# Relu on either of two engines, weighted sums in row halves, and a new order for a fused attention and FFT-gate kernel

## The chip, the cores and the metric

The kernel runs on one core of one Trainium2 chip. The metric is the device time of one execution in microseconds; of several runs the median is given. The core has five engines that work side by side: TensorE (PE, matrix products), VectorE (DVE) and ScalarE (ACT) for elementwise work, GpSimd (POOL) and SyncE (SP), which here start DMAs.

## The reference

For each of 8 batches, with S = 3136 rows, 256 columns and keys of width 64:

```python
scores = (1.0 / S) * np.matmul(z, z.transpose(0, 2, 1))   # z: 8 x 3136 x 64
attn = np.maximum(scores, 0.0) ** 2
x = u * np.matmul(attn, v)                                # u, v: 8 x 3136 x 256

proj = x @ w_proj                                         # 256 x 768
x1, x2, x3 = proj[..., :D], proj[..., D:2*D], proj[..., 2*D:]
X2 = np.fft.rfft(x2, n=S, axis=1)
H = np.fft.rfft(filter_fft, n=S, axis=0)[None, :, :]
y = x1 * np.fft.irfft(X2 * H, n=S, axis=1) * x3
out = y @ w_out
```

All inputs and the output are float32.

## The kernel before

The sequence is cut into 25 tiles of 128 rows (the last has 64) and 7 chunks of columns (five of 512, one of 256, one of 320). A unit is one batch, one chunk and up to four tiles, mostly two. For a unit, PE makes the scores (`score_mm`) into one of three pairs of PSUM banks (`ps_s`). The keys are only 64 wide, so z is kept twice, in the upper and the lower 64 rows, and two score matmuls run side by side on the two row halves of the array. Then `relu` takes the scores out of PSUM into a float32 tile `R_t`, which returns the pair, and `sq` squares `R_t` into the bf16 tile `A_t`. Then PE multiplies `A_t` with v on all 128 rows into two accumulators, `ps_o0` and `ps_o1`, one for each half of the 256 columns (`weigh`). Scores are symmetric, so some squares are transposed by DMA (`mirror`, tiles `M_t`, `M2e_t`, `M2o_t`) and used a second time in place of new scores. The last 64 rows are weighed in half-row matmuls inside score runs (`weigh_short`, which is L1681 in the profile through the helper `by_rows`).

At the end of a chunk DVE multiplies the sums with u (`xT_t`), and the projections follow (`ps_s<-xT_t,wp`), the gates (`gate_t`), and the first step of a Fourier transform of length 3136 = 64 x 49, which goes through DRAM (`spec`) twice. Per batch there are eight transform steps forward and eight inverse, with 64-row matmuls and a product with the filter spectrum H on DVE, and then the last transform step, the gating (`yT_t`) and the output projection.

A planner in the kernel's own code lays out the order before any instruction is emitted. Every piece of work is a `Task` with engines that may run it, assumed costs (`c_act`, `c_dve`, `c_pe`), dependencies and buffer slots. Two strings written out in the code fix what the planner does not choose:

- `ORDER` has one letter for each step on PE: S scores, Q transform steps, W weighted sums on 128 rows, w the first and v the second phase of a weighted sum by row halves, A, B and Z the rest. S, Q, w and v are 64-row work. The string of before holds no w and no v, though the planner knows them.
- `ENGINES` has one letter, a (ACT) or d (DVE), for each task that either engine may do, in the order in which the tasks are made. Before, these are most squares and the evacuations of PSUM; a relu is always on ACT, and the squares of the first chunk behind its first two are always on DVE.

In a w, the row halves 0 and 1 add to different accumulators at the same time (`weigh_rows`); in its v they swap. Where a row half adds to an accumulator that the other half wrote last, `by_rows` puts a wait ahead of it:

```python
dh, at = h ^ flip, slice(h * N1, (h + 1) * N1)
by_rows(
    dh, h, laid(un, acc[dh][ds(m, p), :cw]), row(v16[b], t)[at, ds(dh * P + m, p)], block(un, i, at),
    start=False, stop=False,
)
```

The planner charges 0.096 us for each crossing between 64-row and 128-row work, and 0.235 us (`TURN`) from one phase to the swapped one. Within a DMA's assumed time, constants such as `LATE_TURN` stand for the landing.

The lines of the profile that matter here: L540 every matmul, L1873 the relu, L1880 and L1882 the square on ACT and on DVE, L573 and L577 the evacuations on ACT and on DVE, L1924 the product with u, L1288 the product with H, L1382 the gating, L1681 the half-row sums.

Of the kernel before, what the change touches and what calls it, by code (L numbers as in the profile page):

```python
# [44 lines left out]
    "ASSWBAWSSWAWSASSWSWWSSSWSWSSWWSSSWWWWSWWWWSSSWWWWASSAAWASAAWSAAWWWWWSSWWWWSSBWAWAAAWAWAAWBWSSSWWAWWS"  # L45
    "SSWBWWSBBWWWWBWSSWBWWWAAWSSSWAWBWWAABWWWSSSWWAWWWSSSWWWAWAAAWAAWBASSAAWWSSSWWWWSWWBWWWBWASWWAAWSSWWS"
    "SWABAWWWWASSWAWWAWASSWWAWAWSSSWBAWWSSWAWWBWWAWWSSWAWWAWASSWAWASSAWASSWWSSAWWAQSWWQSSWWWWWQSSWWAAAWAW"
    "SQWAASWAWSSSWAWWQSQWWWSSSWWWWWQSSWWAAWAAAWAWQSSWAWAWSQSWWWWSSSWWWWQSWWWWWWQQQWAASSWAWSAAAWQQWSSQWWWW"
    "WAWASSWAWWASSAWAAAWSSQWAWSQSWWWWAWQSWSWSQWWWWQQSWWWAAWWWASQWWAAAWSQWWWAAWWSSSWWWAAAWSSSWWAWSSSWWSWSS"
    "WWWWSSWWWSWBWBWBWSSSWAAWAASSWAAWASSWBBAWWSSSWWWBWBAWWBSSWAWBWAWSSSWWBBWBWBWBBSSABAWWWBWWBWAAASWAWWWA"  # L50
    "BWSSBWABAWSSABWABAQSSWAWQSWAWSQSWWWWABWBWQSWWAASAWAAWWQSSWABAWSSQWAWQQSWWWSSSWWWWWQSSWWAAWAWAWAQSAWB"
    "QSSWAWAWWQSQWWWWWWSWSWQAWAWWWASSWAWAAWSQSWWAWWASQWWSSWWAASSWWAWWAWSSWSSWWSSWWSSWWWWSSWWBWWWABWSSSWAA"
    "WAASSWBAWBSSBWBAWWSSSWWWWWWSSBAWWABWWAAWSSSWBWBBSBBWAAAWASSBWBSAWBWAWSSWBWBWBWWBAWAAWBWBASABASQBWWAA"
    "BWSQSWWWSSQWWWWWWQSSWWAAAWAWAAWQSSWAABWSSQWWABWSSQWWWWSSQWWWSSSWWWAAWWAAWQSQWAAQSWAWWAWSSQWWWSQWWWSW"
    "QSWWWAWWAAAWWASAWSQAWAWWQSWWSSWWAASSWWWWSSSWAWSSSWWWWWWSSWWWSSWWWBWBABWSSSWAWAAASSWAAWAASSWBBWWABWSS"
    "SWWWWWSSBAWWBWWAASSWABWAASSBWBBAWABAWSSSWBWWBWBWWWSSWWAABWASSWAAAWABWSSQWAWWSBWSQSWBBWBWWWBWWSSQWWAA"
    "AWWSQBAWASQAWBWABWSSQWAWBWQSSWWWWSQSWWWSQSWWWAAAWAAWSQSWAAWWQSSWWAWWWSQSWWWWQQSWWWWWAASQAWAWAAQSWAWA"
    "WWWWSSSWWWAAWAWSSSWWAWSSSWWSSWWWWSSSWWWWWBSBWBWWSSSWAWAASSWAAWBASSWABBWBWWSSSWWAWBAWBWSSABWBWAWBABWA"
    "AAWSSSWAWBSSAWBWWBBWBWAWSSSWWWWSSWAWAWAAAWSSSWABBWABWBBAWQSSWWBWWBWSSQWWWQSWAAWWWASAAWQSABWAWSQSWAWQ"
    "SSWWWWWQSSWWWWSQBWAAWWQSAAWAWQSSWASAWWQSSWWWQQSWWWWWSQWAWAWAWAWWAAWSSQWWAAWWQSSWWWWWSSWWSSWWASSWWSSS"  # L60
    "WWWAWWWWWSSWAAWWWSSWABWSSBAWAAWSSSWBBWSAAWAAWWASSWABWWBBWWBWWAWWSSAAWASSAWABWSSSWABWSSSWBBWWABBWWBWA"
    "BWWWSSSWWBAAWWASSAAAWSQSWBBBWSQSWWWBWWWAWBBWAWQSWBAWASSWWAWSQQWAAWSQSWBAAWWQSWWBWABWSQSWWWWSSQWWWAAW"
    "SQAAWQSAWAAWSQSWAWWSSQWWWWSQSWWWQSWWAWAWAWAAWWQSSWAAWWSSSWWWAWWSSAWWAAWSSWAWSSSWWSWWWSSWWWWWSSSWWBWW"
    "BWBAWSSSWAWASSWAAAWAAWSSSWWWWBWWBBWBWBSSWBAAWWSSSWWAABWSSSWBBWAWAWBBWSSWBWBWWSSSWWAAWWBWBAAWSSQWWWQS"
    "BBWWSQSWWBBWWWWSQSWWBAWWZAWSQSWBABWWSQWSSSWABWWQSQWWWWWBWSSSWAWAWAWQSQWAWWSSQWWQSSWWWWSSSWWWZWWZWWQW"
    "AWSQWQSAAWWWWSSSWWWAWWQSSWWWWWSSSWAWWWWWWAWWWZZAAZAAZZBBBZZBBBZZBBZZZZZZQBQBZBBBQQQQQQQQBQQQQQZQZZZZ"
    "ZZZZZZZBZZZZZZZBZBBBBBBBBBBBBBBBBBBBBBBBBBBBB"
# [3 lines left out]
    "aaddddddddaadddddaaaddddaaddadadadddaadaadaaadaaaadddddddddddaaddadaaadadaddaaadaaadaddaddadaaadddaa"  # L71
    "adadaaaaaaaaddadadddadadaddaddaddddddadadadaaaaddadddaaddadadaaadadddaaadddaaaaddadaddddadaddadddada"
    "aaadddaaaaaaaddddddaddadddaaadaaaaaadadaaaaadaadddddadaddaaaaaaddaaaaddddddddddaaadadaaadaaddddaddaa"
    "addaadaadaaadadadaddadaaaaaddddadadaddddadaadaddddaadddaaaaadaddadddddaadaaadaadaaddaadadaaddaddaada"
    "daaddadaadaaadaadaddddadddaddddaaaddaadaddadddddaddadddaaaaddadaaadaaadadaddddddadaddddaaddaddaaddad"
    "daaaaaaaaaaddadaddddaaadadaaaaadadaddaaaadaaaadaaadadadadaaaadadaadadddddadadadadadddaaaaaaddadadadd"
    "dadddaaadaadadadadddaaaaaddddadaddaddddadaaaaddddaaddaaaadaaadadddadaddadddaadaaaadadaaddaadaaaadaaa"
    "daadadaaaaadaaaddddddddddaaaaaddadddadddaddadadadadddaadddaaaaaaaaaadaaaadadddadadadddadaaaddaaaaaad"
    "adadddddddddaaadaadaaaadadaadadadaaddaaaaddaaaaaaaadadddaaaaddadaddddadadadadadadadadadadaaaadaaddaa"
    "dadddadaadaaaaadaadadddadadaddadddadddaadaddadadddddaaadaaaaadaddadaadaaadaadaddddaaadaaadaadaddaaaa"  # L80
    "daaaaaddaddadaadddddadddaddadddaaddaaddddaadaadddaddaaaaaddaaaadaadaddddadaddaaddaaddadddadaddddadad"
    "daaaadadaaaaaaaaaaaadddadadaaadadadddaaddaaaaaadaaddaadddadaadddaddaadddaaaadaaaaaaaadaaaaaaaadaaaaa"
    "daaaaaaaaaaaadadddaaaaa"
# [14 lines left out]
def c_dve2(n):  # L98
    return 0.068 + n * 0.00052

# [103 lines left out]
class Task:  # L204


    def __init__(self, emit, cost, deps=(), takes=(), prio=0, lat=None, moves=0.0, late=0.0):
        self.emit, self.cost, self.takes, self.prio = emit, cost, list(takes), prio
        self.lat, self.moves, self.late = lat, moves, late
        self.deps = [d if isinstance(d, tuple) else (d, None) for d in deps]  # L210
        self.kids, self.frees = [], []
        self.left = len(self.deps)
        self.ready = 0.0
        self.end = None
        self.holders = 1
        self.second, self.split, self.flips, self.flip = None, False, False, None
        for d, _ in self.deps:
            d.kids.append(self)
# [9 lines left out]
class Plan:  # L228


    def __init__(self):
        self.free = {e: 0.0 for e in ("PE", "ACT", "DVE", "SP", "POOL")}
        self.queues = {"S": [], "Q": [], "W": [], "FA": [], "FB": [], "FZ": []}
        self.pend = {e: [] for e in ("ACT", "DVE", "SP", "POOL")}
        self.mode = None
        self.quarters = False
        self.flip, self.parted, self.turned = None, True, 0.0
        self.rest = []
        self.n = self.at = 0
        self.tasks = []  # L240
        self.spare = []
        self.pairs = None
        self.bus = 0.0

# [31 lines left out]
    def run(self, task, engine, start):  # L276
# [6 lines left out]
        task.end = end  # L283
        task.emit(engine)
# [41 lines left out]
    def pick(self, e):  # L326
        t = self.free[e]
        best = None
        for task in self.pend[e]:
            s = max(t, self.ready_at(task))  # L330
            key = (round(s / 0.03), task.prio, task.no) if s < INF else None
# [79 lines left out]
def kernel(  # L411
# [838 lines left out]
    def add_spectrum(b, puts, early=0):  # L1250
# [10 lines left out]
        for g in range(NJ // 2):  # L1261
# [34 lines left out]
            w_ = on("DVE", lambda mul=mul: mul(0), cost, evs, prio=ZP)  # L1296
            w_ = on("DVE", lambda mul=mul: mul(1), cost, [w_], prio=ZP, lat=ZL)
            z_ = w_ if final else on("DVE", add, 2 * c_dve2(2 * D), [w_], prio=ZP)

# [214 lines left out]
    def casts_at(b, c):  # L1514
# [3 lines left out]
        if n < B and 0 <= i < 4:  # L1518
            t0, t1 = ((0, 8), (8, 16), (16, 22), (22, NT))[i]

            def go_z(tick_):
# [22 lines left out]
                d = on("DVE", dup, c_dve2(P * (t1 - t0)), [a], [zd_p.slots], prio=2)  # L1544
                d.frees.append((a, 0))
# [49 lines left out]
    def m_pool(c, a):  # L1595
        return M_p[0] if a == c + 1 else M_p[1 + c % 2]
# [102 lines left out]
    w_first, w_last = {}, {}  # L1699
# [21 lines left out]
    def add_weigh(un, data, done):  # L1721
        global_k = len(plans[un[:2]])

        def part(dhs):
# [4 lines left out]
            deps = [*data, *cv[b]] if b > 0 and c == 0 else [*data]  # L1729
            t = pe(  # L1730
# [34 lines left out]
    def add_mirrored(un):  # L1765
# [6 lines left out]
        def done(t):  # L1772
            if last:
                t.frees.append((made[0], 0))
# [3 lines left out]
    def mirror(un, q_):  # L1778
# [13 lines left out]
        for a, i, ts in runs:  # L1792
# [3 lines left out]
            def go(a=a, i=i, ts=ts, rows=rows):  # L1796
# [12 lines left out]
                [] if made else [m_pool(c, a).slots], moves=0.78 * len(ts) * cw / 512, late=LATE_TURN,  # L1809
# [26 lines left out]
    for gi, g in enumerate(groups):  # L1836
# [24 lines left out]
        for i, un in enumerate(g):  # L1861
# [8 lines left out]
            def relu(un=un, rows=rows, n=n, cw=cw, box=box):  # L1870
                box["R"] = R_p.tile()
                p = blocks(live[un], n, cw)[:rows]
                has_read(nc.scalar.activation(blocks(box["R"], n, cw)[:rows], p, AF.Relu), p)  # L1873

            def sq(e, un=un, rows=rows, n=n, cw=cw, box=box, a_p=a_p):
# [5 lines left out]
                else:  # L1881
                    nc.vector.tensor_tensor(a, r, r, ALU.mult)  # L1882
# [7 lines left out]
            q_ = job(None, sq, how, [r_], [a_p.slots], prio=1)  # L1890
            q_.frees.append((r_, 0))
# [126 lines left out]
```

## Time and profile before

| | |
|---|---|
| median of 3 runs | 977.86 us (975.88 to 980.27) |
| the profiled execution | 977.09 us, its span 975.3 us |
| PE matmul, weight load | 942.9 us (97%), 468.5 us (48%) |
| DVE, ACT, POOL | 830.5 us (85%), 859.5 us (88%), 201.0 us (21%) |
| granted clock of PE | 0.997 |
| HBM | 147 GB/s over the span |

A row of the profile names the line, the engine and the operation, what is written and read with its shape, the count, the busy time in us and the mean of one in ns, and the idle time of the engine just before with what ended it. In a timeline the first two numbers are the start and the length in us. A matmul's end is modelled, so its pace is read from start to start.

### The profile page before, as it was taken

What the parts mean: (1) busy time and instruction counts of PE and PEld (TensorE: products, weight loads), DVE (VectorE), ACT (ScalarE), POOL (GpSimd) and SP (SyncE); (2) the same over time, 40 slices, a digit from 0 to 9 for tenths busy, and PEclk for the clock granted to TensorE, in tenths of its full rate; (3) what the DMA queues carried; (4) which work ended last, traced back from release to release, by engine and by line L of the source; (5) the groups of instructions that cost most, each with busy time, mean ns of one, the idle gap of its engine ahead of it and who ended that gap; (6) DMA issues with size and microseconds to landing.
All of it is one profiled execution on the core that took longest, in us unless ns stands there. A gap on an engine that the chain in (4) does not pass through costs nothing.

```text
span 975.3 us, 19343 instructions
## 1 busy us (share of the span) xinstructions
PE 942.9 (97%) x6664; PEld 468.5 (48%) x6765; DVE 830.5 (85%) x1492; ACT 859.5 (88%) x1161; POOL 201.0 (21%) x426
## 2 busy tenths in 40 slices
PE   6999999999999999999999999999999999999986
PEld 2344544355544545445444465444545455544654
DVE  8875788999899987898978997799888998889896
ACT  6788898999789999899988999899989999899783
POOL 5142311222012311213111130113201322000031
PEclk9999999999999999999999999999999999999998
DMA  9899899968998788997799997998979977896677
GB/s 156 147 173 176 119 176 159 186 127 152 182 219 176 137 185 179 212 175 151 148 207 189 180 150 173 207 198 155 155 157 206 213 155 152 188 207 143 164 208 241
DMA packets 332403, 170.31 MB, mean 175 GB/s; under 512 B 242598, under 2 KB 307942, under 8 KB 332304
## 3 DMA queue, kind: packets, MB, share of 16 engines
q1 hardware_dynamic: 302496, 132.43, 63.3%
q0 software_dynamic: 29168, 35.13, 24.0%
q10 hardware_dynamic: 640, 1.51, 0.5%
q8 instruction: 53, 0.87, 0.4%
q14 instruction: 46, 0.38, 0.1%
HBM read 90.26 MB, written 53.35 MB: 147 GB/s over the span
## 4 chain that ended last, share of the span: by engine, by line
PE 89%; DVE 4%; ACT 2%; DMA 2%; issue 2%; SPq 0%; ACTq 0%; DVEq 0%
PE ps_o_t L540 51%; PE ps_s L540 36%; ACT R_t L1873 1%; DVE A_t L1882 1%; PE ps_o_t L1681 1%; DMA conv_in_t<-spec 1%; DMA spec_in_t<-spec 1%; DVE yT_t L1382 1%; DMA M2e_t<-A_t 1%; DVE xh L1288 1%; DVE R_t L1288 0%; ACT A_t L1880 0%; DVE gate_t L1196 0%; PE ps_s L543 0%; DVE xT_t L1924 0%
## 5 line engine op out<-in xcount | busy, mean ns | idle before, releaser
L1873 ACT ACTIVATE R_t<-ps_s 128x1024 f32<-128x1024 f32 (+4 forms) x512 | 467.1, 963 | 54.2 <-PE ps_s L540 50.9
L540 PE MATMUL ps_o_t<-A_t,v_t 128*128 128x512 bf16 (+2 forms) x1936 | 441.4, 354 | 10.8 <-issue 4.4
L540 PEld LDWEIGHTS <-v_t 128*128 128x128 bf16 x2706 | 242.8, 98 | 255.2 <-issue 76.9
L1882 DVE TENSOR_TENSOR A_t<-R_t 128x1024 bf16<-128x1024 f32 (+2 forms) x274 | 300.4, 1112 | 30.4 <-ACT R_t L1873 27.1
L1880 ACT ACTIVATE A_t<-R_t 128x1024 bf16<-128x1024 f32 (+4 forms) x222 | 222.3, 1019 | 1.9 <-DMA M2e_t<-A_t 0.9
L540 PE MATMUL ps_s<-zT_t 64*128 64x512 bf16 (+5 forms) x1418 | 161.9, 356 | 1.9 <-DVE zT_t L577 0.5
L623 POOL COPY tick<-xT_t 1x1 bf16<-1x1 bf16 x54 | 14.7, 272 | 688.3 <-DVE xT_t L1924 688.3
L540 PE MATMUL ps_s<-xT_t,wp 128*128 128x512 bf16 (+2 forms) x411 | 104.5, 352 | 1.1 <-DVE gate_t L1196 0.5
L1924 DVE SCALAR_TENSOR_TENSOR xT_t<-ps_o_t,uT_t 128x256 bf16<-128x256 f32 (+2 forms) x224 | 76.0, 382 | 23.1 <-PE ps_o_t L540 18.3
L540 PEld LDWEIGHTS <-zT_t 64*64 64x64 bf16 (+1 forms) x1451 | 50.8, 100 | 91.9 <-issue 77.9
L573 ACT ACTIVATE x_t<-ps_s 128x512 bf16<-128x512 f32 (+2 forms) x126 | 71.8, 587 | 16.5 <-PE ps_s L540 14.7
L1196 DVE TENSOR_TENSOR gate_t<-ps_s,x_t 128x256 bf16<-128x256 f32 (+2 forms) x212 | 71.4, 383 | 17.4 <-PE ps_s L540 12.9
L1288 DVE TENSOR_TENSOR xh<-xh,H 128x1024 bf16<-128x1024 bf16 x120 | 82.1, 684 | 2.7 <-ACT xh L573 1.3
L540 PE MATMUL ps_o_t<-M_t,v_t 128*128 128x512 bf16 (+2 forms) x352 | 81.7, 353 | 0.0
L1382 DVE TENSOR_TENSOR yT_t<-ps_s,gate_t 128x512 bf16<-128x512 f32 (+2 forms) x95 | 57.0, 623 | 12.0 <-PE ps_s L540 11.6
L577 DVE CAST x_t<-ps_s 128x512 bf16<-128x512 f32 (+2 forms) x85 | 52.2, 623 | 12.3 <-PE ps_s L540 6.5
L614 POOL DMA_DIRECT2D un_t<-in_u_dram x112 | 59.9, 557 | 7.6 <-issue 5.7
L540 PEld LDWEIGHTS <-wp 128*128 128x128 bf16 x448 | 41.8, 98 | 39.6 <-issue 7.3
L633 POOL DMA_DIRECT2D v_t<-in_v_dram x112 | 59.4, 555 | 5.2 <-issue 1.9
L540 PE MATMUL ps_s<-wp,xT_t 128*128 128x256 bf16 x396 | 58.0, 273 | 0.2
L540 PE MATMUL ps_s<-wo,yT_t 128*128 128x256 bf16 (+1 forms) x360 | 54.3, 273 | 0.3 <-DVE yT_t L1382 0.2
L577 DVE CAST xh<-ps_s 128x512 bf16<-128x512 f32 x64 | 42.5, 684 | 8.7 <-PE ps_s L540 8.7
(166 smaller groups left out, 871.5 us busy)
## 6 DMA issues: line engine op xcount, KB each, us to landing
out_dram<-ost_t SPq DMA_DIRECT2D x60, 256.0 KB
spec<-s_t SPq DMA_DIRECT2D x96, 128.0 KB
spec_in_t<-spec SPq DMA_DIRECT2D x56, 192.0 KB
spec<-gs_t SPq DMA_DIRECT2D x56, 192.0 KB
v_t<-in_v_dram POOLq DMA_DIRECT2D x80, 128.0 KB, 5.0
un_t<-in_u_dram POOLq DMA_DIRECT2D x80, 128.0 KB, 5.4
conv_in_t<-spec SPq DMA_DIRECT2D x34, 256.0 KB
out_dram<-ost_t SPq DMA_DIRECT2D x18, 128.0 KB
```

The lines of the kernel that those rows point to most:

```text
L540: wrote(nc.tensor.matmul(o, *args, **kw), o)
L573: got = nc.scalar.activation(out_, in_, AF.Copy)
L577: got = nc.vector.tensor_copy(out_, in_)
L614: nc.gpsimd.dma_start(out=t[ds(j * N1, N1), lo - t0 : hi - t0, :], in_=x[:, n2 : n2 + hi - lo, :])
L633: nc.gpsimd.dma_start(out=t[ds(j * N1, N1), ds(v_at(a), (b - a) * D)], in_=r[:, n2 + a - lo : n2 + b - lo, :].rearrange("p t d -> p (t d)"),)
L1196: got = nc.vector.tensor_tensor(g[:, ::-1] if h == 0 else g, p, x, ALU.mult)
L1288: nc.vector.tensor_tensor(x[:, 1 - i], x[:, 0], h, ALU.mult)
L1382: got = nc.vector.tensor_tensor(yb["y"][:, dh, 0:w], p, gates[b, c, dh][:, 0:w], ALU.mult)
L1873: has_read(nc.scalar.activation(blocks(box["R"], n, cw)[:rows], p, AF.Relu), p)
L1880: nc.scalar.activation(a, r, AF.Square)
L1882: nc.vector.tensor_tensor(a, r, r, ALU.mult)
L1924: nc.vector.scalar_tensor_tensor(x, f, inv_s2, ut, ALU.mult, ALU.mult)
```

## The change

- A relu may run on ACT or DVE. `ENGINES` gains a letter for each of the 512 relus, and 11 for squares of the first chunk that were fixed on DVE (1223 to 1746 letters).
- `ORDER` is a new string: 58 W become w, with 58 v (2245 to 2303 letters).
- Three rules of the planner change: a chunk's last weighted sum comes behind the second phases; a mirror's buffer is held until all its weighted sums have read it; and a mirror in the first chunk of the first batch is assumed to land 2.0 us later.
- GpSimd gets a price for a square, but is taken off the list again in the next line; `ports` and `port` are read only for GpSimd squares.

The two strings are shown by their first line only:

```diff
 ORDER = (
-    "ASSWBAWSSWAWSASSWSWWSSSWSWSSWWSSSWWWWSWWWWSSSWWWWASSAAWASAAWSAAWWWWWSSWWWWSSBWAWAAAWAWAAWBWSSSWWAWWS"
...
+    "ASBSWASWSWASWwSASvWSwSSWvwSSvSWSwSvSWWWWSSWWWWSSWWWWWSwSvSAWSAAAWAWAWWWBWSSWWAWWSAWWBSSAWWBSSwSvwSvA"
...
 ENGINES = (
-    "aaddddddddaadddddaaaddddaaddadadadddaadaadaaadaaaadddddddddddaaddadaaadadaddaaadaaadaddaddadaaadddaa"
...
+    "aaddddddddaaadddadaaaaaaadadaadaddaaadaadaaaaadadadadadadadadadaaadddaaddaaadddaadaaadaddaaddaaadaaa"
...
+def c_pool(n):
+    return 0.12 + n * 0.00173
...
+            if k == len(plans[b, c]) - 1:
+                deps += [(x, ISSUED) for x in seconds.get((b, c), ())]
...
+                seconds.setdefault((b, c), []).append(after_it)
...
         def done(t):
-            if last:
-                t.frees.append((made[0], 0))
+            if not last:
+                made[0].holders += 1
+            t.frees.append((made[0], 0))
...
-                [] if made else [m_pool(c, a).slots], moves=0.78 * len(ts) * cw / 512, late=LATE_TURN,
+                [] if made else [m_pool(c, a).slots], moves=0.78 * len(ts) * cw / 512, late=LATE_TURN + 2.0 * (b == c == 0),
...
-            def relu(un=un, rows=rows, n=n, cw=cw, box=box):
+            def relu(e, un=un, rows=rows, n=n, cw=cw, box=box):
                 box["R"] = R_p.tile()
                 p = blocks(live[un], n, cw)[:rows]
-                has_read(nc.scalar.activation(blocks(box["R"], n, cw)[:rows], p, AF.Relu), p)
+                r = blocks(box["R"], n, cw)[:rows]
+                if e == "ACT":
+                    has_read(nc.scalar.activation(r, p, AF.Relu), p)
+                else:
+                    has_read(nc.vector.tensor_single_scalar(r, p, 0.0, ALU.max), p)
...
-            r_ = on(
-                "ACT", relu, c_act(n * cw), [(st, -sum(costs[i + 1 :]) - extra)], [R_p.slots], prio=0
+            r_ = job(
+                None, relu, both(n * cw), [(st, -sum(costs[i + 1 :]) - extra)], [R_p.slots], prio=0
             )
...
-            how = {"DVE": c_dve(n * cw)} if (b, c) == (0, 0) and k > 1 else {"DVE": c_dve(n * cw), "ACT": c_act(n * cw) + 0.039}
+            how = {"DVE": c_dve(n * cw), "ACT": c_act(n * cw) + 0.039, "POOL": c_pool(n * cw)}
+            del how["POOL"]
```

More of the change, by code (lines that the diff above doesn't have):

```diff
@@ L50 @@
[L50 to L64, printed above, removed]
@@ L68 @@
+    "BBB"
 )
 ENGINES = (
-    "aaddddddddaadddddaaaddddaaddadadadddaadaadaaadaaaadddddddddddaaddadaaadadaddaaadaaadaddaddadaaadddaa"
[L72 to L80, printed above, removed]
@@ L215, in __init__ @@
         self.holders = 1
+        self.ports = ()
         self.second, self.split, self.flips, self.flip = None, False, False, None
@@ L243, in __init__ @@
         self.bus = 0.0
+        self.port = {"DVE": 0.0, "POOL": 0.0}
     def add(self, task, kind=None):
@@ L283, in run @@
         task.end = end
+        if engine in task.ports:
+            self.port[engine] = end
         task.emit(engine)
@@ L330, in pick @@
             s = max(t, self.ready_at(task))
+            if e in task.ports:
+                s = max(s, self.port["POOL" if e == "DVE" else "DVE"])
             key = (round(s / 0.03), task.prio, task.no) if s < INF else None
@@ L1544, in go_z @@
                 d = on("DVE", dup, c_dve2(P * (t1 - t0)), [a], [zd_p.slots], prio=2)
+                d.ports = ("DVE",)
                 d.frees.append((a, 0))
@@ L1697, in weigh_rows @@
                     )
-    w_first, w_last = {}, {}
+    w_first, w_last, seconds = {}, {}, {}
     def weigh(un, dhs):
```

55 lines of the change are left out of this document (44 added, 11 removed).

## The prediction

> **What bounds the kernel now.** I read the page first: the busy shares, then the chain that ended last.
>
> ```profile
> span 975.3 us, 19343 instructions
> PE 942.9 (97%) x6664; PEld 468.5 (48%) x6765; DVE 830.5 (85%) x1492; ACT 859.5 (88%) x1161; POOL 201.0 (21%) x426
> PE 89%; DVE 4%; ACT 2%; DMA 2%; issue 2%; SPq 0%; ACTq 0%; DVEq 0%
> ```
>
> TensorE (PE) works 97% of the span and holds 89% of the chain. VectorE (DVE) and ScalarE (ACT) are near 86% each, so they are busy but not the bound on average. An average can hide a stage, so I asked for the busy time by stage, cut at the first matmul, at the end of the set-up, and at the end of the score work:
>
> ```profile
> 0.00:4.00 4.00, 0.00 (x0) 0.00 (x0) 2.28 (x18) 1.34 (x2) 3.27 (x13) 1.00 0.43 80
> 4.00:30.00 26.00, 21.75 (x110) 8.13 (x112) 21.05 (x40) 19.50 (x27) 10.00 (x24) 1.00 1.20 173
> 30.00:60.00 30.00, 28.21 (x146) 12.03 (x150) 27.64 (x52) 24.56 (x32) 7.50 (x15) 1.00 0.85 142
> 60.00:915.00 855.00, 846.31 (x5937) 418.53 (x6029) 732.29 (x1290) 780.34 (x1041) 168.01 (x353) 1.00 0.88 173
> 915.00:976.00 61.00, 46.65 (x476) 29.79 (x476) 47.27 (x97) 33.71 (x65) 12.26 (x23) 0.95 0.75 225
> ```
>
> After the length of the stage, the columns are PE, weight loads, DVE, ACT and POOL. From 60 to 915 us PE is idle for 8.7 of 855 us: seven eighths of the kernel run at PE's own pace, and shifting work between ACT and DVE cannot shorten them unless PE itself gets less to do. The idle time of PE that could go is 4.2 us before 30, 1.8 us before 60, 8.7 us in the middle, and 14.4 us after 915, the last of which includes the stores after the final matmul.
>
> Whether "busy" hides stalls is seen from start to start in PE's timeline:
>
> ```profile
> 264.56 1.89 PE L540 MATMUL ps_o_t<-A_t,v_t 128*128 128x512 bf16 x8
> 266.29 0.39 PE L540 MATMUL ps_s<-T,conv_in_t 128*128 128x128 bf16 x4
> ...
> 275.38 1.03 PE L540 MATMUL ps_o_t<-M_t,v_t 128*128 128x512 bf16 x4
> 276.34 0.61 PE L540 MATMUL ps_s<-zT_t 64*128 64x512 bf16 x4
> 276.88 0.61 PE L540 MATMUL ps_s<-xT_t,wp 128*128 128x512 bf16 x2
> ...
> 262.50 0.39 PE L540 MATMUL ps_s<-zT_t 64*128 64x512 bf16 x2
> 262.73 0.38 PE L1681 MATMUL ps_o_t<-As_t,v_t 64*128 64x512 bf16 x2
> 262.94 0.38 PE L540 MATMUL ps_s<-zT_t 64*128 64x512 bf16 x2
> 263.25 0.61 PE L540 MATMUL ps_s<-xT_t,wp 128*128 128x512 bf16 x2
> ```
>
> Eight full matmuls take 266.29 - 264.56 = 1.73 us, 0.216 each, which is the pace. Four of them would take 0.86 us, but the score run behind 275.38 starts after 0.96: crossing from 128 rows to 64 rows costs 0.10. Its four matmuls go two at a time (2 x 0.216 = 0.43), and the next full matmul starts after 0.54: crossing back costs 0.11. So a run of 64-row work costs about 0.2 us in crossings, whatever it holds. The rows at 262.73 are a weighted sum by row halves inside such a run: 0.23 and 0.21 us from start to start for a pair, no more than the score pairs around it.
>
> **The change, part by part.**
>
> *Fewer crossings.* In the string ORDER the letters S, Q, w, v are 64-row work and the rest is full. Counting changes between the two kinds gives 548 before and 528 after (274 and 264 runs). That is 20 x 0.10 = 2.0 us less, directly on PE. The matmul work itself does not change: a weighted sum of two tiles is four full matmuls, 4 x 0.216 = 0.86 us, and as two phases it is four pairs, also 4 x 0.216.
>
> *The phases.* 58 of the 928 weighted-sum steps become a w and a v. The second phase lets each row half add to the sum that the other half has just written, and it waits for that. Following the string, the halves swap within a run 26 times: 13 times with one score or transform unit between, 13 times with two or more; never with none. In 22 other cases the second phase begins in a new run, behind full matmuls, and in the remaining 10 it meets no swap. The trace of before has no swap. Its nearest bound from below is 0 (the pair at 262.73 shows no premium); from above it is the part of a matmul that outlasts the pace, 0.38 - 0.216 = 0.16 us, with no cover by the unit between: 26 x 0.16 = 4.2 us. I take 0.8 us, nearer to zero, because a unit of 0.216 lies between and is longer than the 0.16.
>
> [...]
>
> *Relus and squares.* I walked the steps in the order in which the code makes them and read the two engine strings along. Of 512 relus, 161 go to DVE (120 of 1024 elements, 32 of 640, 9 smaller). 93 squares go the other way, from DVE to ACT (DVE 286 to 193), and 52 evacuations net as well.
>
> ```profile
> L1873 ACT ACTIVATE R_t<-ps_s 128x1024 f32<-128x1024 f32 x408 | 403.0, 1035 | 47.8 <-PE ps_s L540 45.2 <-DVE xh L577 0.5 <-DVE A_t L1882 0.5
> L1873 ACT ACTIVATE R_t<-ps_s 128x640 f32<-128x640 f32 x72 | 47.9, 710 | 4.9 <-PE ps_s L540 4.3 <-DVE xT_t L1924 0.2
> L1882 DVE TENSOR_TENSOR A_t<-R_t 128x1024 bf16<-128x1024 f32 x208 | 251.3, 1218 | 21.9 <-ACT R_t L1873 18.6 <-DMA M2e_t<-A_t 2.3
> L1882 DVE TENSOR_TENSOR A_t<-R_t 128x640 bf16<-128x640 f32 x52 | 41.4, 820 | 8.3 <-ACT R_t L1873 8.2
> L1882 DVE TENSOR_TENSOR A_t<-R_t 128x512 bf16<-128x512 f32 x7 | 4.8, 682 | 0.0
> L1880 ACT ACTIVATE A_t<-R_t 128x1024 bf16<-128x1024 f32 x184 | 195.6, 1078 | 1.7 <-DMA M2e_t<-A_t 0.9
> L577 DVE COPY ost_t<-ps_s 128x512 f32<-128x512 f32 x29 | 19.8, 685 | 6.2 <-PE ps_s L540 2.4 <-issue 1.7 <-ACT ost_t L573 1.2
> L579 DVE TENSOR_SCALAR H<-ps_s 128x512 bf16<-128x512 f32 x8 | 5.3, 684 | 1.8 <-PE ps_s L540 1.8
> L573 ACT ACTIVATE ost_t<-ps_s 128x512 f32<-128x512 f32 x49 | 29.7, 611 | 9.4 <-PE ps_s L540 9.3
> ```
>
> A relu on DVE does not occur before. The same kind of instruction from PSUM (L579) takes 684 ns for 512 elements, a float copy from PSUM 685; another 512 elements cost 1218 - 682 = 536, so 1.22 us for 1024, and 0.82 for 640 by the square of that size. DVE gains 120 x 1.22 + 32 x 0.82 + about 6 for the nine = 179 us, and loses 93 squares (1.11, the mean over its shapes: 251.3 + 41.4 + 4.8 us over 267) = 104 and 52 evacuations x 0.685 = 36: 830.5 becomes about 870, 89%. ACT loses 120 x 1.035 + 32 x 0.71 + about 5 = 152, gains 93 x 1.02 + 52 x 0.61 = 127: 859.5 becomes about 834, 86%. So the two engines swap places, and their sum grows by some 14 us. Neither becomes the bound, and in the middle all of it lies beside PE's matmuls. Its cover is the idle tenth of each engine; where that is gone PE waits (second rival). What it can buy is that two relus run at once and a PSUM pair comes back up to 1 us earlier. PE's idle 8.7 us in the middle sets the limit; most of it is edges of many short pieces, so I take 0.5 us of it, with bounds of -3 and +6.
>
> *The start.*
>
> ```profile
> DVE A_t L1882 <- DMA M2e_t<-A_t: 2.3, 1, 2.3
> PE ps_o_t L540 <- DVE xT_t L1924: 2.0, 1, 2.0
> PE ps_o_t L540 <- DVE A_t L1882: 2.0, 1, 2.0
> 24.51 4.99 DMA M2e_t<-A_t
> ```
>
> The chain has DVE A_t, then 4.99 us of the DMA transpose into M2e, then DVE again at 29.6: the squares stood still for a buffer that the transpose was reading, and PE lost 2.0 us behind it. The diff adds 2 us to the assumed landing of the mirrors of the first chunk (LATE_TURN + 2.0 where b and c are 0), so the new order is laid out round the late landing. I take 1.5 of the 2.0 us (bounds 0 and 2.0). The other 2.0 us, PE behind the first squares, fall where DVE also runs the set-up. The squares of the first chunk, fixed on DVE, may now go to ACT, and the first two do. I take 1.2 us (bounds -2.0 and +1.5). What is late next is ACT, which had 4.00 + 26.00 - 1.34 - 19.50 = 9.2 us free there.
>
> *The end.* The last batch's transforms hold no relu, and DVE is what is full there:
>
> ```profile
> 925.00:940.00 15.00, 12.50 (x144) 8.32 (x147) 13.74 (x26) 10.34 (x20) 4.24 (x8) 1.00 0.78 232
> ```
>
> In its string three evacuations just ahead leave DVE and three later ones join it. I take 0, with 3 us either way. The waits added for the last phase (seconds) and the holders of the mirror slots only order work on PE that stands in that order anyway. The POOL price (c_pool, ports) is dead: the choice is deleted again in the next line.
>
> **The sum.** -2.0 + 0.8 - 0.5 - 1.5 - 1.2 + 0 = -4.4 us. The profiled execution took 977.09 us (span 975.3 and 1.8 around it), so 972.7; the median of the runs shown is 977.86, 0.8 above it, so I forecast **973.5 us**. With the bounds taken together loosely, this case runs from 967 to 981.
>
> **Rivals.**
>
> *Two drains do more.* ACT waits for PE 50.9 us in total before relus:
>
> ```profile
> ACT R_t L1873 <- PE ps_s L540: 50.9, 76, 2.7
> ```
>
> That is time in which the pair ahead was already free. It speaks against a shortage of pairs, and so against this rival; for it speaks that runs of up to fourteen letters now occur. If a third of the middle's idle goes and 3 us at the end, the time is 973.5 - 2.9 - 3 = 967.6. Chance 0.17.
>
> *The swaps drain uncovered.* PE's sequencer may hold even the units between, because the wait stands ahead of them in one queue. A whole matmul time per swap is 26 x 0.38 = 9.9 us in place of 0.8: 982.6. It turns the gain into a loss from 0.2 us per swap on. The pair at 262.73 neither shows nor excludes it. Chance 0.07.
>
> *Relus stuck behind DVE work (slower).* DVE goes to 89%, and its queue is in order. A relu there stands behind a square or relu of 1.22 us: half of that, 0.6 us, if it comes at a random moment. Where PE's next score step needs that pair, PE waits as long, since its order is fixed. 7 such cases of the 161 eat up the 4.4 us, and 16 make the kernel slower by over 0.5%. At one in seven, 23 x 0.6 = 13.8 us, it is 987. For it: the free share is now only a tenth on both sides. Against it: the same squares on DVE at 1.22 us left PE unhindered in the middle. Chance 0.17.
>
> That the change does nothing in the middle, because PE is the bound, is inside the forecast: of the 4.4 us only 1.7 come from there.
>
> **How the numbers follow.** 0.5% is 4.9 us, about what a measurement of this kernel can tell from no change: faster is below 973.0, slower above 982.7. The forecast has 0.59: 0.25 below 973.0, 0.33 within, 0.01 above. The first rival gives 0.17 faster, the second 0.04 within and 0.03 slower, the third 0.01 within and 0.16 slower. So faster 0.42, same 0.38, slower 0.20. The range runs from below the first rival, 963, to the third, 987.
>
> **What would show it.** Right: PE's idle time from 60 to 915 stays under 10 us, and the count of weight loads held back at crossings falls with the runs; relus on DVE read 1.22 us; no wait for M2e near 25 us; pieces of w and v follow a score pair after 0.21 to 0.23 us. Wrong: a new line "PE ps_s from DVE R_t" with tens of us, a gap of 0.3 us or more ahead of second phases, or a longer stage behind 915.

## The result, and the profile after

No difference that can be measured. The changed kernel takes 977.27 us (median of 12 runs, 974.37 to 981.76), the kernel before in the same comparison 977.18 (12 runs, 975.63 to 980.27): a ratio of 1.0004, 95% interval 0.9987 to 1.0021. The profiled execution took 977.31 us. The page of the changed kernel, span, engines and chain:

```profile
span 975.5 us, 20058 instructions
PE 950.4 (97%) x7097; PEld 469.8 (48%) x7097; DVE 870.8 (89%) x1508; ACT 836.0 (86%) x1145; POOL 197.4 (20%) x426
PE 85%; DVE 6%; DMA 5%; issue 1%; ACT 1%; SPq 1%; POOL 0%; ACTq 0%; DVEq 0%; POOLq 0%
```

DVE and ACT have changed places. In the chain the DMAs' share rises from 2% to 5%. That is not the start, where the chain holds 4.5 us of DMA (u's transpose) against 5.0 before (the one into M2e); it is the middle and the end, with 4.6 us at 315 us for a load of z that comes up again below. The busy time by stage, with the same cuts and columns as before:

```profile
0.00:4.00 4.00, 0.00 (x0) 0.00 (x0) 2.28 (x18) 1.34 (x2) 3.26 (x13) 1.00 0.41 87
4.00:30.00 26.00, 20.58 (x122) 7.56 (x124) 19.54 (x38) 20.07 (x26) 10.16 (x23) 1.00 1.18 160
30.00:60.00 30.00, 27.45 (x153) 10.61 (x150) 27.41 (x48) 22.99 (x27) 7.51 (x15) 1.00 0.82 141
60.00:915.00 855.00, 853.34 (x6336) 420.79 (x6334) 773.91 (x1310) 755.53 (x1024) 164.20 (x353) 1.00 0.90 173
915.00:976.00 61.00, 49.05 (x495) 30.86 (x490) 47.66 (x97) 36.03 (x69) 12.22 (x23) 0.96 0.76 225
```

PE's idle time grows at the start, from 4.2 to 5.4 us before 30 and from 1.8 to 2.6 us from 30 to 60. In the middle it falls from 8.7 to 1.7 us, but that is not 7 us won. The page of before counts 6664 matmuls to 6765 weight loads, so some 100 matmul records are missing from that trace, and a missing record looks like idle time; here both counts are 7097. What can be compared is the time at which both programs have done the same steps. From the starts of the weight loads in the two profiles:

```
us                            before    changed
step 129 / 137 of ORDER        73.10      76.29
step 2145 / 2203 of ORDER     920.61     922.27
between the two               847.51     845.98
from there to ORDER's end      45.85      44.69
```

So in these two profiles the new order comes out of the start 3.2 us late, gains 1.5 us in the long middle and 1.2 us in the last stage. How much of that a second profile repeats is seen in the experiments.

### The profile page after: what moved, and what is told of

Its sections match the earlier page's. It is cut to its first block, busy times and chain, and to the rows that moved or that the text cites. A ratio compares the mean times of both kernels' runs of the same rounds, so it can differ in the third digit from the quotient of the medians.

```text
span 975.5 us, 20058 instructions
## 1 busy us (share of the span) xinstructions
PE 950.4 (97%) x7097; PEld 469.8 (48%) x7097; DVE 870.8 (89%) x1508; ACT 836.0 (86%) x1145; POOL 197.4 (20%) x426
## 4 chain that ended last, share of the span: by engine, by line
PE 85%; DVE 6%; DMA 5%; issue 1%; ACT 1%; SPq 1%; POOL 0%; ACTq 0%; DVEq 0%; POOLq 0%
PE ps_o_t L556 45%; PE ps_s L556 35%; PE ps_o_t L1701 5%; DMA zn_t<-in_z_dram 1%; DVE A_t L1910 1%; DMA conv_in_t<-spec 1%; DVE R_t L1901 1%; DMA gs_t<-spec 1%; DMA spec_in_t<-spec 1%; DVE yT_t L1401 1%; DVE xh L1304 0%; DVE xT_t L1954 0%; DMA uT_t<-un_t 0%; DVE gate_t L1212 0%; DMA spec<-s_t 0%
## 5 line engine op out<-in xcount | busy, mean ns | idle before, releaser
L556 PE MATMUL ps_o_t<-A_t,v_t 128*128 128x512 bf16 (+2 forms) x1832 | 420.6, 356 | 3.8 <-DVE xT_t L1954 1.9
L1899 ACT ACTIVATE R_t<-ps_s 128x1024 f32<-128x1024 f32 (+2 forms) x351 | 328.3, 967 | 56.7 <-PE ps_s L556 51.8
L556 PEld LDWEIGHTS <-v_t 128*128 128x128 bf16 x2462 | 221.7, 98 | 231.6 <-issue 68.6
L1908 ACT ACTIVATE A_t<-R_t 128x1024 bf16<-128x1024 f32 (+3 forms) x310 | 301.8, 991 | 17.7 <-DVE R_t L1901 12.8
L1910 DVE TENSOR_TENSOR A_t<-R_t 128x1024 bf16<-128x1024 f32 (+3 forms) x186 | 207.5, 1128 | 10.1 <-ACT R_t L1899 7.1
L1901 DVE TENSOR_SCALAR R_t<-ps_s 128x1024 f32<-128x1024 f32 (+3 forms) x161 | 176.9, 1108 | 22.9 <-PE ps_s L556 17.4
L556 PE MATMUL ps_s<-xT_t,wp 128*128 128x512 bf16 (+2 forms) x422 | 110.4, 353 | 0.3 <-DVE R_t L1901 0.3
L556 PEld LDWEIGHTS <-zT_t 64*128 64x128 bf16 (+1 forms) x1388 | 51.6, 99 | 90.8 <-issue 70.6
L556 PE MATMUL ps_o_t<-M_t,v_t 128*128 128x512 bf16 (+2 forms) x320 | 73.5, 353 | 0.0
L1701 PE MATMUL ps_o_t<-A_t,v_t 64*64 64x512 bf16 (+4 forms) x562 | 56.7, 350 | 0.0
```

The lines of the kernel that those rows point to most:

```text
L556: wrote(nc.tensor.matmul(o, *args, **kw), o)
L1701: row_sums[dh] = h, nc.tensor.matmul(*args, **kw)
L1899: has_read(nc.scalar.activation(r, p, AF.Relu), p)
L1901: has_read(nc.vector.tensor_single_scalar(r, p, 0.0, ALU.max), p)
L1908: nc.scalar.activation(a, r, AF.Square)
L1910: (nc.vector if e == "DVE" else nc.gpsimd).tensor_tensor(a, r, r, ALU.mult)
```

## Experiments

Two theories stood against each other. The first: PE's own work sets the time, the new strings take 2 us of crossings from it, and what happens at the start and the end decides the rest. The second: the moved relus cost several us by themselves, which the better order wins back, so that nothing is left. All kernels below compute the whole reference. Ratios are to the kernel before, with 95% intervals.

**e1: no phases.** In the changed kernel's ORDER every w becomes a W and every v is dropped; the crossings rise from 528 to 596.

```diff
-    "ASBSWASWSWASWwSASvWSwSSWvwSSvSWSwSvSWWWW...
+    "ASBSWASWSWASWWSASWSWSSWWSSSWSWSSWWWW...
```

> The changed kernel with each of its 58 weighted sums by row halves made whole again (w becomes W, v goes; the rest of both strings stays). Crossings between 64-row and 128-row work go from 528 to 596. Ledger theory (PE is the bound, each crossing costs 0.10 us, swaps are covered): 68 x 0.10 = 6.8 us more than the changed kernel, about 984 us. Rival (the phases cost as much as the crossings that they save): within 2 us of the changed kernel, 975 to 979.

Measured: 1002.86 us, 1.0255 (1.0217 to 1.0293). That is 25.6 us over the changed kernel, not 6.8. From the waits of the whole run, the weight loads held back at crossings (511 in the changed kernel):

```profile
PEld L555 <- issue: 225.9, 637, 1.6
```

And PE's longest kind of wait from 60 to 915 us, where the changed kernel waits 1.6 us in all:

```profile
PE ps_s L555 <- ACT R_t L1898: 2.9, 4, 1.4
```

The crossings explain 68 x 0.10 = 6.8 us. One gap of 2.08 us at 693 us and one at 950 also lowered the clock (to 0.76 over the 7 us behind each, below), 1.7 us each. PE's waits that have a row come to 24.3 us in all, against 15.9 in the changed kernel, and lie on many rows. That leaves 7 us of the 25.6 without a row. What is shown is that this order with these letters cannot do without its phases; that they give the relus time between scores is my reading, not shown.

**e2: the new order with all relus on ACT.** The changed kernel's ORDER, with ENGINES of before (an a at each relu).

```diff
 ENGINES = (
-    "aaddddddddaaadddadaaaaaaadadaadaddaaadaad...
+    (the letters of before, and an a for each of the 512 relus)
```

> The changed kernel's PE order with the engines of before: all relus on ScalarE, squares and evacuations where they were. Ledger theory (the middle is PE's own pace, but the new order needs the two engines): PE has the same work and crossings, and what is added is PE waiting for a second relu behind the first: 0 to 5 us more than the changed kernel, 977 to 982. Rival (moved relus hold PE up by several us, which eat up what the new order saves): 970 to 974.

Measured: 1037.89 us, 1.0621 (1.058 to 1.0661), 60 us over the changed kernel and far more than expected. From its waits over the whole run:

```profile
DVE A_t L1910 <- ACT R_t L1899: 59.5, 58, 3.2
PE ps_s L556 <- ACT R_t L1899: 15.4, 27, 1.5
```

DVE is only 80% busy and stands 59.5 us for relus that ACT has not done yet (7.1 in the changed kernel); PE then stands for the pair. The second theory has the sign wrong: without its relus on DVE the new order is slower by far. But the letters of before were laid out for another order, so this run does not yet price a relu's place.

**e9: only the place of relus, at equal load.** In 101 units with the relu on DVE and the square on ACT the two letters are exchanged. `ORDER`, and the number of instructions on each engine, stay; the planner lays the queues out anew round the letters, so the order on DVE, ACT and SP moves with them, and on PE some transform and output steps change places (112 of 7097 weight loads).

```diff
-  relu of the unit: d, its square: a     (101 units)
+  relu of the unit: a, its square: d
```

> The changed kernel with 101 units turned round: where the relu is on VectorE and the square on ScalarE, the relu goes to ScalarE and the square to VectorE. Both engines keep their load within 3 us a unit class (DVE 1.22 to 1.22, ACT 1.08 to 1.04), and both strings stay otherwise. If the order needs two relus at once (a PSUM pair back about 1 us earlier), PE waits in the middle for R_t on ACT and the kernel is 15 to 40 us slower, 992 to 1017. If only the engines' load counts: within 3 us of the changed kernel.

Measured: 1009.65 us, 1.0303 (1.0266 to 1.0339). The loads on its page:

```profile
PE 964.3 (96%) x7097; PEld 474.1 (47%) x7097; DVE 872.3 (87%) x1508; ACT 834.5 (83%) x1145; POOL 198.0 (20%) x426
```

And of its waits over the whole run, the row of DVE in the changed kernel, then DVE's and two of PE's in e9:

```profile
DVE A_t L1910 <- ACT R_t L1899: 7.1, 11, 1.5
```

```profile
DVE A_t L1910 <- ACT R_t L1899: 35.5, 44, 3.4
PE ps_s L556 <- ACT R_t L1899: 6.2, 17, 1.1
PE ps_s L556 <- DMA conv_in_t<-spec: 6.5, 3, 3.7
```

DVE and ACT are as busy as in the changed kernel to within 2 us, and the kernel is 32 us longer. What counts is which engine takes which relu, not how busy the two are: 60 relus are left on DVE in place of 161, and the busy shares of 87% and 83% say nothing of it. The way from the letters to the 32 us is shown only in part. PE's waits with a row grow from 15.9 to 31.9 us, of which 6.2 are for relus on ACT and 6.5 (1.3 in the changed kernel) for a load of the transform; 3.4 us are two clock falls (0.76 over 7 us) behind gaps of 3.75 and 2.52 us (last section); some 13 us have no row. And no run exchanges 101 other letters, so it is open whether relus are special here, or whether any letters that were not laid out together with this `ORDER` would cost as much.

**e3 and e5: the planner's rules alone.** e3 gives both strings of before (an a at each relu) to the changed planner; e5 takes the 2.0 us of assumed landing back out.

```diff
-... late=LATE_TURN + 2.0 * (b == c == 0),
+... late=LATE_TURN,
```

> Both strings of before under the planner of after (late landing of the first mirrors, held mirror buffers, order of second phases). Ledger theory: the time of before within 1.5 us, 975.5 to 979; the start may differ by the order of SP's queue. Rival (the planner's rules alone move the time, and the strings are neutral): more than 3 us from before.

> The changed kernel without the 2.0 us on the landing of the first mirrors. With both strings fixed, every engine's instructions come out in the same order as in the changed kernel, so it is the same program. If the start theory holds (the new strings are no faster because their start loses, by waits for DMA transposes that differ from run to run, what the middle and the end gain): 977 us within 1.5, the letters behind the first 60 us in the same times within 0.1 us, and the first 60 us different by up to 4 us. Rival (the assumed landing itself cost the start 2 to 3 us): 974 to 975.

Measured: e3 979.25 us, 1.0013 (0.9994 to 1.0033); e5 980.29 us, 1.0007 (0.9986 to 1.0028). e3 turns out to be instruction for instruction the program of before, e5 that of the changed kernel. The three rules do nothing here; the strings are the whole change. The two runs are worth keeping as repeats: by the marks used above, e5 spent 75.4, 848.0 and 48.1 us in the three parts where the changed kernel's profile had 76.3, 846.0 and 44.7, and e3 spent 77.3, 847.3 and 46.8 where that of before had 73.1, 847.5 and 45.9. The same program varies by up to 4.2 us in a part, and e3, which is the program of before, comes to the first mark later than the changed kernel did. So the 3.2 us at the start cannot be read from two profiles.

**e4: swaps without cover.** In 20 of the 26 swaps inside a run the second phase is put directly behind the first.

```diff
-... wSSvWWSSS ...
+... wvSSWWSSS ...
```

> The changed kernel with the second phase set directly behind the first where both lie in one run: 20 of the 26 swaps lose the unit that lay between, nothing else moves in the two strings. If a swap has to wait for the end of the last matmul and the unit between is its cover: 20 x 0.16 to 0.40 = 3 to 8 us more than the changed kernel, 980 to 985. If a swap is free by itself: the changed kernel's time within 1.5 us.

Measured: 984.17 us, 1.0075 (1.0049 to 1.0102), 6.9 us over the changed kernel. A covered swap in the changed kernel's timeline, then a bare one in that of e4:

```profile
24.61 0.59 PE L1701 MATMUL ps_o_t<-A_t,v_t 64*128 64x512 bf16 x4
25.04 0.38 PE L556 MATMUL ps_s<-zT_t 64*128 64x512 bf16 x2
25.27 0.61 PE L1701 MATMUL ps_o_t<-A_t,v_t 64*128 64x512 bf16 x4
```

```profile
25.15 1.27 PE L1701 MATMUL ps_o_t<-A_t,v_t 64*128 64x512 bf16 x8
25.81 0.11 PEld L1701 LDWEIGHTS <-v_t 64*128 64x128 bf16 x4 [0.56 <-PE ps_o_t L1701]
26.25 0.60 PE L556 MATMUL ps_s<-zT_t 64*128 64x512 bf16 x4
```

With a score pair between, the second phase starts 0.23 us behind that pair: the pace. Bare, the four pairs take 26.25 - 25.15 = 1.10 us where the pace is 4 x 0.216 = 0.86: 0.24 us for the swap, between the two prices that the prediction had for it (0.16 and 0.38). The covered row is typical: in the changed kernel's trace 18 weight loads of half-row sums wait for another half-row sum; 14 of them have 512 columns of scores ahead of them, and there the matmul starts 0.22 to 0.23 us after the one ahead every time. 20 x 0.24 = 4.8 of the 6.9 us; this profile also has PE at one pair for 2.9 us where the changed kernel's has 1.1, with a clock fall behind it (0.78 over 7 us).

**e6 and e8: one more buffer.** A ninth tile for the squares, and one fewer for xT_t, while the planner still counts eight of each: on the changed kernel (e6) and on before (e8).

```diff
-    A_p = Pool("A", 8, [P, 1024], BF16)
+    A_p = Pool("A", 9, [P, 1024], BF16)
+    A_p.slots = Slots(8)
```

> The changed kernel with 9 buffers for the squares in place of 8 (and 7 for xT in place of 8, of which no more than 7 are held at once); the planner still counts 8, so every order stays. Start theory: squares no longer stand still for a transpose that reads their buffer near 26 to 33 us, 1 to 3 us less, 974 to 976. Rival (the start is held by u's transpose behind the mirrors in SP's queue, or by PE's accumulators): within 1 us of the changed kernel.

> The kernel before with the 9 and 7 buffers of the other run; orders as before. Start theory: its wait of 4.99 us for the transpose into M2e, 2.0 us of it on PE, goes: 1 to 3 us less than before, 974 to 976. Rival (the wait moves to the next user of the same transpose): within 1 us of before.

Measured: e6 978.82 us, 1.0004 (0.9985 to 1.0023); e8 979.62 us, 1.0009 (0.9989 to 1.003). No effect that can be measured.

**e7, e10: u's transpose first.** At the start SP's queue holds the mirrors ahead of u's transpose. In the timelines, SP's DMA transposes of the changed kernel and DVE's and PE's first wait for them:

```profile
19.04 8.59 SPq L1829 DMA_TRANSPOSE M2e_t<-A_t  x2
27.73 3.61 SPq L1513 DMA_TRANSPOSE uT_t<-un_t  x2
32.34 0.76 DVE L1954 SCALAR_TENSOR_TENSOR xT_t<-ps_o_t,uT_t 128x256 bf16<-128x256 f32 x2 [2.44 <-DMA uT_t<-un_t]
33.24 0.59 PE L556 MATMUL ps_o_t<-A_t,v_t 128*128 128x512 bf16 x2 [1.89 <-DVE xT_t L1954]
```

e7 issues the first of u's two transposes ahead of the second mirror; e10 adds e6's buffers. The lines that call it:

```diff
+                if (b, c, a) == (0, 0, 2) and (b, c, a) in mirrors:
+                    ahead_u[0, 0]()
```

> The changed kernel with u's transpose for the first chunk issued by SP ahead of the second transpose into M2e, not behind it; nothing else moves. In the changed kernel DVE waited 2.44 us for it and PE 1.89 us behind that. If that wait sets the start: 0.9 to 1.9 us less, 975.4 to 976.4. Rival (the late squares of the same time set it): within 0.5 us of the changed kernel.

> The changed kernel with both repairs of its start: nine buffers for squares, and u's first transpose ahead of the second one into M2e. If the waits of the start are what is left between the new strings and a gain: 2 to 4 us less than before, 974 to 977 where before is 979. If the start's waits only change places: within 1 us of the run with the transpose alone, 977 to 979.

Measured: e7 977.73 us against 979.21 of before on that chip, 0.9982 (0.9962 to 1.0002); e10 978.99, 1.0001 (0.9982 to 1.0021). e5, the changed program on the chip of e7, took 980.29: 2.6 us more by the medians, 1.9 by the means, with an interval of some 2.2 us either way. In e7's profile u's transpose comes earlier, and DVE does not wait for it:

```profile
23.16 1.25 SPq L1517 DMA_TRANSPOSE uT_t<-un_t  x1
28.08 0.75 DVE L1961 SCALAR_TENSOR_TENSOR xT_t<-ps_o_t,uT_t 128x256 bf16<-128x256 f32 x2
```

DVE has xT_t 4.3 us earlier than in the changed kernel's profile. The first mark comes at 73.1 us (73.2 in e11, which has the same edit), against 76.3, 75.4 (e5) and 75.1 (e12) without it. But e6, without it, came to 73.7, and e10, with it, to 77.3. In e10 the waits are there all the same, and the clock fell behind PE's (0.76 over 7 us):

```profile
DVE xT_t L1963 <- DMA uT_t<-un_t: 2.7, 1, 2.7
PE ps_o_t L558 <- DVE xT_t L1963: 2.2, 1, 2.2
```

What goes with the mark is the moment at which SP is done with its first transpose into M2e, whatever the edit: 23.1, 23.1 and 23.2 us in e6, e7 and e11, but 25.1, 25.4, 26.3 and 27.0 in e12, e5, the changed kernel and e10. So 2.6 of the 4.3 us are the luck of that profile: e6 has xT_t at 29.75 us without the edit. Where that moment is the same, the edit is worth about 0.6 us (e6 against e7 and e11), and the time is not clear of before.

**e11, e12: one stall in the middle.** Near 320 us PE waits for a pair in each profile of the changed program. DVE's timeline there, and PE's wait:

```profile
319.47 0.36 DVE L1550 COPY zd_t<-zn_t 128x768 bf16<-128x768 bf16 x1 [2.04 <-DMA zn_t<-in_z_dram]
319.75 0.68 DVE L1304 TENSOR_TENSOR xh<-xh,H 128x1024 bf16<-128x1024 bf16 x1
320.35 1.22 DVE L1901 TENSOR_SCALAR R_t<-ps_s 128x1024 f32<-128x1024 f32 x1
321.62 0.39 PE L556 MATMUL ps_s<-zT_t 64*128 64x256 bf16 x4 [1.09 <-DVE R_t L1901]
```

A copy at the head of DVE's queue waits 2.04 us for a load of z, and the relu that gives PE its pair stands two places behind it and comes only after it. e12 makes the planner assume that this one load lands later, which moves the copy seven places back and leaves the order on PE, ACT and POOL; e11 has this and e7's edit.

```diff
-... moves=0.09 * (t1 - t0), late=LATE_CAST)
+... moves=0.09 * (t1 - t0), late=LATE_CAST + 2.0 * (n == 3 and t0 == 16))
```

> The edit of e7 (u's transpose first) and one more: the assumed landing of one load of z (batch 3, its third part) is 2.0 us later, so the planner puts VectorE's copy of it (zd_t) six instructions later in VectorE's queue, behind two relus; the order on PE, ScalarE and GpSimd stays. In every run of the new program VectorE stood 2.0 to 3.2 us at that copy near 319 us, and PE stood 1.1 to 2.3 us at a pair whose relu was queued behind it. Theory (the few stalls over 1 us, and the clock that falls behind some of them, are what is left to gain): PE's wait for R_t near 320 us goes, the granted clock stays 1.00 from 310 to 335 us in every profile, and the time falls by 1 to 3 us below e7 (ratio to before 0.995 to 0.998). Rival (such a stall only uses up slack that shows later at another wait): the wait goes, another of the same size comes within 20 us, and the time is that of e7 or of before (0.998 to 1.001).

> The new program with the later assumed landing of that one load of z alone (without e7's edit). Theory: PE's wait near 320 us goes, the start stays as it is (PE waits near 31 us for xT_t behind u's transpose), and the time falls by 1 to 3 us against the new program (ratio to before 0.997 to 1.000). Rival: no change (1.000 to 1.001). Beside the run with both edits it also gives the worth of u's transpose by a second pair: 1 to 3 us if the first reading (1.8 us) holds, 0 if that was chance.

Measured, against 978.61 us of before on that chip: e11 976.69 us, 0.9975 (0.9954 to 0.9995); e12 977.20 us, 0.9988 (0.9963 to 1.0013). From the busy time by stretch, the changed kernel and then e11 (the first count is PE's):

```profile
320.00:330.00 10.00, 8.91 (x70) 4.38 (x68) 9.29 (x16) 8.78 (x13) 0.18 (x1) 1.00 0.90 110
```

```profile
320.00:330.00 10.00, 9.95 (x89) 5.61 (x89) 8.46 (x18) 9.79 (x15) 4.06 (x9) 1.00 0.67 119
```

PE's wait is gone in e11 as in e12, and none took its place near it. From the first mark to the second e11 takes 843.8 us and e12 844.2, where before's program takes 847.3 to 848.6 in three profiles (before, e3, e8) and the changed one, with the stall, 845.6 to 848.0 in five. The upper end of e11's interval is below 1: it is the one version here that beats the kernel before, by a quarter of a per cent and by a narrow margin, among thirteen comparisons with it. It was not run side by side with the changed kernel, and the two single effects (e7, e12) are not clear of noise by themselves.

## Why the prediction was right, and where it was wrong

The forecast was 973.5 us in 963 to 987, the result is 977.27: inside the range, but within 0.5% of before, to which it gave 0.38 against 0.42 for faster. The range is 24 us wide, and it is this width that holds the result: the gain of 4.4 us did not come. Step by step:

*Crossings, -2.0: right.* The weight loads held back at crossings, of the changed kernel against 199.2 us and 557 times before:

```profile
PEld L556 <- issue: 184.4, 511, 2.4
```

PE goes on beside such a hold (it is 97% busy with 199 us of them), so the price is read from start to start. It holds over the whole trace of the changed kernel: behind a matmul of 512 columns the next one starts after 0.216 us within 128-row work (median of 2007), 0.311 into 64-row work (174) and 0.312 back (207). Counted from the weight loads' order, the crossings that were run fall from 550 to 532: 18 x 0.10 = 1.8 us. They fall in the middle alone, from 496 to 468, and rise from 42 to 48 ahead of the first mark and from 12 to 16 behind the second.

*Phases, +0.8: right in kind, a little too dear.* Covered swaps run at 0.22 to 0.23 us, so they cost close to nothing. The rival in which the swaps drain uncovered would have needed them bare; a bare one costs 0.24 (e4). So in e4 the wait ahead of a second phase takes 0.24 us, and in the changed kernel one unit of 0.216 us between the phases hides it.

*Loads: right.* 870 and 834 us were forecast for DVE and ACT, 870.8 and 836.0 came. The relu on DVE, from the groups by form, forecast at 1.22 and 0.82 us:

```profile
L1901 DVE TENSOR_SCALAR R_t<-ps_s 128x1024 f32<-128x1024 f32 x120 | 145.2, 1220 | 19.7 <-PE ps_s L556 15.6 <-ACT H L591 1.5 <-ACT A_t L1908 1.2
L1901 DVE TENSOR_SCALAR R_t<-ps_s 128x640 f32<-128x640 f32 x32 | 26.0, 819 | 3.1 <-PE ps_s L556 1.8 <-ACT A_t L1908 1.0
```

*Middle, -0.5: its bounds held, its reasoning did not.* The three middle terms made -1.7 us, and -1.5 is what the marks show in the first two profiles (845.6 to 848.0 against 847.3 to 848.6 over all). But the 8.7 us of idle time from which the -0.5 was taken were not there: in e3, the same program with all of its records, PE is busy for all but 0.1 us of this stretch.

```profile
60.00:915.00 855.00, 854.86 (x6015) 417.74 (x6015) 732.31 (x1288) 779.81 (x1037) 168.03 (x353) 1.00 0.90 173
```

What PE has less of there are the 28 crossings, 2.8 us, and 1.1 to 2.3 us are given back at one stall. That stall is the third rival, the relu behind DVE work (the part on relus and squares calls it the second), at a single place and not at one relu in seven. PE's whole wait for relus on DVE in the middle:

```profile
PE ps_s L556 <- DVE R_t L1901: 1.4, 2, 1.1
```

Nor was it the square ahead of the relu, as that rival had it, but a copy that waited for a DMA. And the place of the relus was put down as a small bonus ("two relus run at once"). e9 shows that the new order stands on it: 32 us hang on which relus go to DVE. That it is two relus at once that does it is not shown.

*M2e wait, -1.5, and the rest of the start, -1.2: wrong, and the largest part of the miss.* The two waits that were to go did go, but others took their places. DVE no longer waits for M2e. "What is late next is ACT" names the smaller part of what followed: in the changed kernel's profile PE loses 1.0 and 0.6 us behind squares, of which the first waits on ACT for a transpose, and e5 and e12 do not show this. The larger part, and in all three, is u's transpose, which stands in SP's queue behind mirrors that take it 8.59 us: DVE waits 2.44 us for it and PE 1.89 (1.6 and 1.8 in e5 and e12). And the 1.95 us that PE waited for the first squares became 1.59 us for a table of the set-up (`T`) and 0.79 for a transposed part of z, in every profile of the changed program: the new `ORDER` has its first B earlier. The edit on which the step leaned, 2.0 us more assumed landing, changes no instruction (e5).

Whether the start even lost is seen when the end of both transposes into M2e is set beside the marks (the row of SP before, then all profiles in which they stand next to each other in its queue):

```profile
19.15 6.62 SPq L1805 DMA_TRANSPOSE M2e_t<-A_t  x2
```

```
us                                before      e3      e8 changed      e5     e12      e6
SP is done with M2e                25.77   28.35   24.68   27.63   26.77   26.46   24.44
first mark                         73.10   77.29   71.86   76.29   75.44   75.13   73.70
from the one to the other          47.33   48.94   47.18   48.66   48.67   48.67   49.26
```

SP takes 6.62 us for them in before and 9.24 in e3, the same program, so their end is a matter of the run. From there before's program needs 47.2 to 47.3 us (e3's 48.9 hold a clock fall of 1.7), the changed one 48.7 or more. So of the 3.2 us between the first two profiles about 1.4 belong to the new order, of which six more crossings make 0.6, and 1.8 are chance. The two terms promised -2.7 us; the start came out about 1.4 us worse. A moved wait has to be followed through every queue it shares, and the queue here was SP's.

*End, 0: not contradicted.* The part behind the second mark takes 45.9 to 48.3 us in the three profiles of before's program and 44.3 to 48.9 in the seven of the changed one, e7, e10, e11 and e12 included. The 1.2 us of the first two profiles are less than one program varies.

The first rival, two drains that do more, asked for 5.9 us less in the middle and at the end; the marks of the first two profiles show 2.7, and there are 3.7 in the middle alone once the stall at 320 us is out (847.5 to 843.8 in e11). Of the signs named ahead, PE's idle time under 10 us could tell nothing, since before showed it too, and for a start that loses elsewhere than at M2e there was none.

**What remains open.** The new order gains 1 to 2 us in the middle and loses about as much at the start, as far as ten profiles can show it; the end is lost in what one program varies. Over 12 runs the sum is 0 with an interval of 1.7 us either way. Why SP's transposes take 2.6 us longer in one run than in another of the same program is not known, and neither is what makes 0.8 us of the start's 1.4, nor where 7 us of e1 and 13 us of e9 go.

## What to carry to other kernels

When an order on the bounding engine is fixed, ask for each relu, copy or evacuation what stands ahead of it in its queue and whether that can wait for a DMA: one such copy held PE up for 1.1 to 2.3 us in every profile of the changed program, where the covered second phases ran at the pace (0.22 to 0.23 us). Busy shares tell little about where work should go; exchanging two letters in 101 units at the same load cost 3%. When a wait is laid out away, list what else its queue holds at that moment; here the next in that queue was the new wait. And before a difference between two single profiles is explained, look at a second profile of the same program: one stage differed by 4.2 us here.

## What the runs showed of the hardware

The clock of PE fell behind gaps of only 2 us. The granted clock in the changed kernel's profile around its gap of 1.09 us at 320 us, and in e10's around its gap of 2.06 us at the same place (length, busy times, then the clock as the third number from the end):

```profile
320.53:321.62 1.09, 0.00 (x1) 0.00 (x0) 1.09 (x2) 0.49 (x2) 0.00 (x0) 1.00 1.06 81
321.62:328.62 7.00, 7.00 (x53) 3.38 (x53) 6.53 (x11) 6.38 (x9) 0.00 (x0) 1.00 0.85 107
```

```profile
321.50:323.50 2.00, 0.00 (x0) 0.00 (x0) 2.00 (x4) 0.46 (x1) 0.00 (x0) 1.00 1.16 189
323.55:330.55 7.00, 7.00 (x43) 3.14 (x46) 5.44 (x9) 4.87 (x6) 0.00 (x0) 0.76 0.78 116
```

For 7 us behind the gap of 2.06 us the clock is 0.76 on average, and PE starts 43 matmuls in place of 53. 0.24 x 7 = 1.7 us are lost on top of the gap. The rows of PE's waits give eight gaps of 2.06 to 3.75 us later than 14 us (two each in e9 and e10, one each in e1, e4, e5 and e12), and each has such a fall behind it (0.76 over 7 us, 0.78 in e4). Of the gaps from 1.4 to 1.9 us, 1.89 in the changed kernel, 1.8 in e6 and in e12 and 1.4 in e7 have none (1.00 over 7 us); in e2, where PE's longest wait from 60 to 915 us is 1.5 us, the clock is 0.76 from 122.59 to 129.59 us all the same. e11 shows a fall (0.66 from 930 to 935 us) behind two shorter gaps close together, 0.96 and 0.69 us. Gaps ahead of 14 us are not counted: there matmuls of 512 columns within 128-row work start 0.38 to 0.43 us apart in the profiles of before and of the changed kernel, against 0.216 as the median of the whole trace. A gap of 1.96 us (2.0 in the rows of before and e3) went both ways. Before and e3 are one program; the stretch from 35 to 40 us behind such a gap, which ended at 31.6 us in before and at 34.2 in e3, where shorter gaps of 1.29 and 0.73 us stood close ahead of it:

```profile
35.00:40.00 5.00, 4.95 (x27) 1.84 (x26) 5.00 (x7) 4.42 (x7) 0.85 (x2) 1.00 1.07 146
```

```profile
35.00:40.00 5.00, 5.00 (x20) 1.68 (x19) 5.00 (x7) 3.07 (x3) 2.47 (x5) 0.66 0.56 69
```

So a gap of 1.96 us cost about 2 us in before and 1.7 more in e3, and what decides between the two is not shown. This goes along with the spread between runs: of the 99 runs of before's program beside the experiments, the 19 at a mean clock of 0.998 average 977.3 us, the 13 at 0.994 average 981.4, and the groups between lie in between.
